# Sparse attention and an ELU layer on one core: x^T in the order of the tokens, local scores written with a step, output tiles of 128 neighbouring rows

## The chip, the cores and the metric

The kernel runs on one core of one Trainium2 chip. The metric is the device time of one execution in microseconds. Three runs of the kernel before gave 311.32 (median), 312.10 and 311.09 us. The profile of before is of one further execution, of 311.37 us.

## The reference

Eight batches of eight heads, 576 positions of 64 numbers each. The first four heads are local (a query sees itself and the 31 keys before it), the last four strided (a query sees the keys at or before it whose position has the same remainder by 32). The heads of a position are then put side by side to a row x of 512 numbers, and 4608 such rows go through two dense layers with an ELU between them.

```python
scores = scale * np.matmul(q, k.transpose(0, 1, 3, 2))
mask_local = (rel >= 0) & (rel < 32)
mask_strided = (rel >= 0) & (pos[None, :] % 32 == pos[:, None] % 32)
attn = np.exp(scores - max) / sum          # masked, per row
x = (attn @ v).transpose(0, 2, 1, 3).reshape(B * S, H * D)
h = x @ w_in                                # 512 -> 2048
g = np.where(h > 0, h, np.exp(np.minimum(h, 0.0)) - 1.0)
return g @ w_out                            # 2048 -> 512
```

Inputs and output are float32; the kernel computes its matmuls in bf16.

## The kernel before, in words

**Residues.** A batch's 576 positions are looked at as 72 groups p of NS = 8 neighbours s, position = 8p + s. Strided heads only mix positions of equal remainder by 8 (by 32 within it, by a mask), so their scores are eight blocks of 72 x 72 (RS = 72), one for each s. Local heads are cut into LB = 6 blocks of LQ = 96 queries, each against 128 keys (its own 96 and the 32 before).

**x^T.** The attention result is kept as `xT[128, 4, 4608]` in bf16, feature by token, all 4608 tokens in SBUF. Feature slices 0 and 1 are the local heads, 2 and 3 the strided. Within a batch its columns are in the order (s, p): column 72s + p holds position 8p + s. The dense layers don't mind the order of the tokens, so only the store has to undo it.

**Attention steps**, for a batch, a kind (s or l), a pair of heads y and a half u. T and c/C transpose q and k and copy them to `qT`, `kT` (batches from 3 on get them by a transposing DMA, X). q lies in `qT` in the order (s, p) for both kinds, keys of local heads in natural order. `scores` (S, L464) makes 8 matmuls of 72 columns (strided) or 6 of 96 columns (local), two at a time: one on rows 0 to 63 into one PSUM bank and one on rows 64 to 127 into another. Of a local block the 96 columns go to eight pieces of 12 neighbouring words (`local_cols`: order (s, block, p)). `exp_s` (e, L471, ScalarE) and `mask` (m, L478 strided, L484 local, VectorE) give the weights `pm`. `pv` (O) multiplies with V and with ones: for batches 0 and 1 in `pv_old` (L491 to L512), for the others in `pv_new` (L527 strided, L534 local; the local one reads and writes pieces of 12). `log_sums` and `recip` (n and r, L562 and L568, ScalarE) make 1 / sum as exp(-ln). `write_x` (x, L593, VectorE) multiplies the product in PSUM by it and writes x^T: 64 instructions, 32 strided that write contiguous columns and 32 local that write eight pieces of 36.

**Dense layers**, in nine chunks of 512 tokens. `l1` (a, b, L; L623): for each of 16 blocks of 128 hidden features, four matmuls of 512 columns over the feature slices in the order 2, 3, 0, 1. Then `exp_h` (h, L631, ScalarE), `clamp` (i on VectorE, L640, or j on ScalarE, L638), `elu` (g, L649 or L651, VectorE). `l2` (Z; L657): for each tile of 128 tokens, 16 matmuls of 512 columns over the hidden blocks. `copy_o` (o on ScalarE, q on VectorE; L663) brings the tile to SBUF, with four buffers, and `store` (t; L675) sends it to DRAM. The last tile is made in two halves of 256 columns (`l2_half` L683, `out_half` L696 to L700), whose last half goes out over SP and ACT.

**Stores.** A tile of 128 columns of x^T runs through two or three residues s, and the rows of one residue lie 8 rows apart in the output. So `store` sends each tile as 2 or 3 transfers, of up to 72 rows of 2 KB each.

**The order.** Nothing schedules itself: `ORDER` is a list of 1396 tokens written out ahead, each a step with its arguments (`S.3l1.0.34`: scores of batch 3, local, pair 1, half 0, into banks 3 and 4; `Z.2.1.0.2`: second layer of chunk 2, tile 1, quarter 0, bank 2). Every engine takes its instructions in that order, and waits by semaphores for operands, buffers and banks. All eight PSUM banks are given out by these tokens. Batch 0's attention comes first (the head), then stretches of first-layer blocks (h, i or j, g beside them) alternate with stretches in which second-layer quarters are mixed with the attention of later batches. q, k and v are loaded by POOL's queue (D), transposing DMAs (X) and stores share SP's queue.

Of the kernel before, what the change touches and what calls it, by code (L numbers as in the profile page):

```python
# [9 lines left out]
BF16 = mybir.dt.bfloat16  # L10
# [37 lines left out]
D.wo3.0 b.0.7 g.0.8 T.1s1.q.2 h.0.7 a.0.3.6 c.1s1.q T.1s0.k.1 C.1s0.q a.0.15.4 g.0.9 D.qs.2 C.1s0.k
T.1s1.k.2 i.0.7 b.0.15 c.1s1.k S.1s0.1.01 h.0.15 g.0.7 b.0.3 D.ks.2 e.1s0.1 b.0.14 i.0.15 h.0.3
g.0.15 T.1l1.q.7 S.1s0.0.01 h.0.14 m.1s0.1 S.1s1.0.45 D.ql.2 e.1s0.0 i.0.3 a.0.12.2 i.0.14 b.0.12  # L50
e.1s1.0 m.1s0.0 T.1l0.q.0 g.0.14 h.0.12 T.1l0.k.1 O.1s0.0.45 D.kl.2 C.1l0.q m.1s1.0 a.0.10.3 i.0.12
n.1s0.0 g.0.3 T.1l1.k.0 r.1s0.0 b.0.10 C.1l1.k x.1s0.0 a.0.13.6 g.0.12 h.0.10 O.1s0.1.45 C.1l0.k
c.1l1.q b.0.13 D.vs.2 V.1 n.1s0.1 S.1l1.0.12 h.0.13 Z.0.2.0.7 i.0.10 e.1l1.0 g.0.10 Z.0.1.0.0
r.1s0.1 m.1l1.0 j.0.13 x.1s0.1 S.1l0.1.12 g.0.13 O.1l1.0.34 D.vl.2 e.1l0.1 Z.0.2.1.7 n.1l1.0 m.1l0.1
r.1l1.0 Z.0.1.1.0 x.1l1.0 S.1l0.0.12 S.1s1.1.34 S.1l1.1.56 e.1l0.0 Z.0.2.2.7 e.1l1.1 m.1l0.0
Z.0.1.2.0 e.1s1.1 m.1l1.1 O.1l1.1.56 O.1l0.0.34 n.1l1.1 O.1s1.0.12 n.1l0.0 Z.0.2.3.7 m.1s1.1 n.1s1.0
r.1l0.0 r.1l1.1 Z.0.1.3.0 x.1l0.0 o.0.2 x.1l1.1 r.1s1.0 Z.0.0.0.3 t.0.2 o.0.1 x.1s1.0 Z.0.0.1.3
t.0.1 Z.0.0.2.3 Z.0.0.3.3 O.1s1.1.12 o.0.0 O.1l0.1.67 n.1s1.1 T.2s1.q.0 t.0.0 T.2s1.k.3 n.1l0.1
c.2s1.q r.1s1.1 T.2l0.k.5 c.2s1.k T.2l0.q.4 r.1l0.1 T.2l1.k.0 x.1s1.1 C.2l0.k T.2l1.q.3 x.1l0.1
S.2s1.0.12 C.2l1.k W.2 T.2s0.q.5 L.1.13.6 e.2s1.0 D.qs.3 c.2s0.q C.2l1.q c.2l0.q T.2s0.k.7 m.2s1.0  # L60
L.1.6.5 h.1.13 D.ks.3 V.2 j.1.13 c.2s0.k L.1.11.4 D.vs.3 h.1.6 g.1.13 D.ql.3 S.2s0.0.23 i.1.6 h.1.11
S.2l0.1.01 L.1.10.6 g.1.6 e.2s0.0 X.qs.3 i.1.11 e.2l0.1 L.1.8.7 m.2s0.0 h.1.10 g.1.11 O.2s0.0.01
h.1.8 L.1.5.2 m.2l0.1 i.1.10 n.2s0.0 i.1.8 O.2s1.0.34 X.ks.3 Z.0.3.0.5 g.1.10 r.2s0.0 g.1.8 h.1.5
Z.0.3.1.5 x.2s0.0 n.2s1.0 L.1.4.7 r.2s1.0 i.1.5 D.kl.3 g.1.5 L.1.7.6 h.1.4 x.2s1.0 Z.0.3.2.5 h.1.7
i.1.4 L.1.1.4 i.1.7 g.1.4 L.1.0.3 g.1.7 h.1.1 i.1.1 L.1.12.7 h.1.0 g.1.1 D.vl.3 X.ql.3 L.1.2.6 i.1.0
# [685 lines left out]
```

## Time and profile before

| | us |
|---|---|
| median of three runs | 311.32 |
| profiled execution | 311.37 |
| its span, first to last instruction | 309.4 |
| PE (matmuls) busy | 297.2 |
| ScalarE busy | 233.7 |
| VectorE busy | 223.4 |
| POOL busy | 74.8 |
| first-layer matmuls, L623 | 129.6 |
| second-layer matmuls, L657 | 128.9 |
| scores, L464, from 10 to 300 us | 15.2 |
| writes of x^T, L593 | 42.4 |

The span of a profile runs from the first to the last instruction of the core; what the execution takes beyond it lies around it. PE is TensorE's matmuls and PEld its weight loads, which overlap them; DVE is VectorE, ACT ScalarE, POOL GpSimd, SP SyncE, which here only issues DMAs. The durations of matmuls overlap too: one of 512 columns is shown with some 380 ns, while the next starts 216 ns later. So the cost of a matmul in a stream is read from the length of a row of several: its length less the duration of the last, by the number less one. A row of the timeline is start, length, engine, line, operation, tiles and shape, count, and in brackets how long the engine was idle before it and who released it. Some matmul records are missing in a trace.

### The profile page before, as it was taken

What the parts mean: (1) busy time and instruction counts of PE and PEld (TensorE: products, weight loads), DVE (VectorE), ACT (ScalarE), POOL (GpSimd) and SP (SyncE); (2) the same over time, 40 slices, a digit from 0 to 9 for tenths busy, and PEclk for the clock granted to TensorE, in tenths of its full rate; (3) what the DMA queues carried; (4) which work ended last, traced back from release to release, by engine and by line L of the source; (5) the groups of instructions that cost most, each with busy time, mean ns of one, the idle gap of its engine ahead of it and who ended that gap; (6) DMA issues with size and microseconds to landing.
All of it is one profiled execution on the core that took longest, in us unless ns stands there. A gap on an engine that the chain in (4) does not pass through costs nothing.

```text
span 309.4 us, 6379 instructions
## 1 busy us (share of the span) xinstructions
PE 297.2 (96%) x2374; PEld 151.6 (49%) x2412; DVE 223.4 (72%) x445; ACT 233.7 (76%) x410; POOL 74.8 (24%) x104
## 2 busy tenths in 40 slices
PE   5989999999999999999999999999999999999994
PEld 5754545544554455444544544455444544444443
DVE  6869972999669976898689679946798359990100
ACT  4769976979887899887998997879886767881211
POOL 8933310761084048003810082000000000000000
PEclk9559999999999999999999999999999999999999
DMA  8999999999999999994999589222200220002222
GB/s 161 189 206 206 195 206 213 165 133 152 151 200 161 123 201 183 106 125 87 190 155 122 119 113 159 47 67 71 68 3 0 70 68 1 0 2 57 67 79 70
DMA packets 96952, 36.29 MB, mean 117 GB/s; under 512 B 77754, under 2 KB 92442, under 8 KB 96922
## 3 DMA queue, kind: packets, MB, share of 16 engines
q0 software_dynamic: 64608, 19.40, 61.0%
q1 hardware_dynamic: 31878, 16.09, 28.9%
q10 hardware_dynamic: 436, 0.40, 0.5%
q8 instruction: 19, 0.31, 0.4%
q14 instruction: 11, 0.09, 0.1%
HBM read 39.41 MB, written 9.44 MB: 158 GB/s over the span
## 4 chain that ended last, share of the span: by engine, by line
PE 72%; DVE 15%; DMA 6%; issue 4%; ACT 2%; DVEq 0%; ACTq 0%
PE ps L657 34%; PE ps L623 27%; DVE g L651 6%; DMA vl<-in_v_dram 5%; DVE he L640 5%; PE ps L464 3%; PE ps L527 2%; PE ps L534 2%; DVE xT L593 1%; DMA g<-in_k_dram 1%; DVE g L649 1%; PE ps L683 1%; PE ps L421 1%; PE ps L418 1%; ACT he L631 1%
## 5 line engine op out<-in xcount | busy, mean ns | idle before, releaser
L623 PE MATMUL ps<-xT,w_in_sb 128*128 128x512 bf16 x560 | 129.6, 381 | 1.5 <-DVE g L651 0.4
L657 PE MATMUL ps<-w_out_sb,g 128*128 128x512 bf16 x538 | 128.9, 379 | 1.8 <-issue 1.0
L631 ACT ACTIVATE he<-ps 128x512 f32<-128x512 f32 x144 | 84.5, 594 | 23.3 <-PE ps L623 21.0
L623 PEld LDWEIGHTS <-w_in_sb 128*128 128x128 bf16 x576 | 55.1, 98 | 65.3 <-issue 2.3
L657 PEld LDWEIGHTS <-g 128*128 128x128 bf16 x560 | 50.6, 98 | 53.4
L651 DVE TENSOR_TENSOR g<-he,ps 128x512 bf16<-128x512 bf16 x112 | 74.0, 681 | 1.5
L640 DVE TENSOR_SCALAR he<-he 128x512 bf16<-128x512 f32 x112 | 46.3, 431 | 16.2 <-ACT he L631 15.7
L593 DVE TENSOR_TENSOR xT<-ps,ln 64x576 bf16<-64x576 f32 (+1 forms) x64 | 42.4, 678 | 21.6 <-ACT ln L568 21.1
L471 ACT ACTIVATE e<-ps 128x576 bf16<-128x576 f32 (+1 forms) x64 | 39.4, 646 | 5.8 <-PE ps L464 5.0
L562 ACT ACTIVATE ln<-ps 64x576 f32<-64x576 f32 (+1 forms) x64 | 36.3, 584 | 5.8 <-PE ps L527 2.6
L568 ACT ACTIVATE ln<-ln 64x576 f32<-64x576 f32 (+1 forms) x64 | 38.7, 620 | 1.4
L663 ACT COPY osb<-ps 128x512 f32<-128x512 f32 x27 | 15.8, 585 | 29.1 <-PE ps L657 26.1
L232 POOL DMA_DIRECT2D vs<-in_v_dram x8 | 5.3, 662 | 71.7 <-DVE vsp L603 69.4
L478 DVE TENSOR_TENSOR pm<-e,mask_s 72x576 bf16<-72x576 bf16 x32 | 14.4, 451 | 11.3 <-ACT e L471 10.8
L649 DVE SCALAR_TENSOR_TENSOR g<-he,ps 128x512 bf16<-128x512 bf16 x32 | 21.7, 680 | 0.6
L638 ACT ACTIVATE he<-he 128x512 bf16<-128x512 f32 x32 | 20.1, 627 | 0.7
L484 DVE TENSOR_TENSOR pm<-e,mask_l 128x576 bf16<-128x576 bf16 x32 | 14.5, 456 | 5.4 <-ACT e L471 4.4
L238 POOL DMA_DIRECT2D ql<-in_q_dram x20 | 16.3, 821 | 0.5 <-issue 0.4
L245 POOL DMA_DIRECT2D kl<-in_k_dram x20 | 15.5, 801 | 1.2 <-DMA vs<-in_v_dram 0.9
L527 PEld LDWEIGHTS <-vsp 72*128 72x128 bf16 x192 | 9.1, 98 | 5.8 <-DVE vsp L603 0.7
L700 DVE COPY osb<-ps 128x128 f32<-128x128 f32 x1 | 0.3, 291 | 15.0 <-ACT osb L699 15.0
L534 PEld LDWEIGHTS <-vl 128*128 128x128 bf16 x144 | 8.2, 97 | 4.4
(87 smaller groups left out, 176.4 us busy)
## 6 DMA issues: line engine op xcount, KB each, us to landing
out_dram<-osb SPq DMA_DIRECT2D x31, 144.0 KB
w_out_sb<-in_moe_w_out_dram POOLq DMA_DIRECT2D x4, 512.0 KB, 15.4
vl<-in_v_dram POOLq DMA_DIRECT2D x7, 288.0 KB, 6.6
qs<-in_q_dram POOLq DMA_DIRECT2D x5, 320.0 KB, 9.5
ks<-in_k_dram POOLq DMA_DIRECT2D x5, 320.0 KB, 11.2
vs<-in_v_dram POOLq DMA_DIRECT2D x5, 320.0 KB, 6.0
w_in_sb<-in_moe_w_in_dram POOLq DMA_DIRECT2D x3, 512.0 KB, 11.2
ql<-in_q_dram POOLq DMA_DIRECT2D x20, 72.0 KB, 6.9
```

What stands on the lines that cost most here:

```text
L238: nc.gpsimd.dma_start(out=t[0:RS, h % 2, :, h // 2, :], in_=q[b, h].rearrange("(p s) d -> p s d", s=NS))
L471: nc.scalar.activation(e[0:R], tiles.pop(("S", key, u))[0:R], ACT.Exp, scale=scale)
L562: nc.scalar.activation(t, s_ps, ACT.Ln)
L568: nc.scalar.activation(t, t, ACT.Exp, scale=-1.0)
L593: nc.vector.tensor_mul(dst, o_ps, rc)
L623: nc.tensor.matmul(tiles["h", ch, m], lhsT=w_in_sb[:, c, m * 128:(m + 1) * 128], rhs=xT[:, c, ch * CHUNK:(ch + 1) * CHUNK], start=(c == 2) ...
L631: nc.scalar.activation(e, tiles["h", i[0], i[1]], ACT.Exp)
L638: nc.scalar.activation(e1, e, ACT.Relu, bias=1.0, scale=-1.0)
L640: eng.tensor_scalar(e1, e, scalar1=1.0, scalar2=1.0, op0=ALU.min, op1=ALU.subtract)
L649: nc.vector.scalar_tensor_tensor(dst, e1, -1.0, h, op0=ALU.mult, op1=ALU.max)
L651: nc.vector.tensor_tensor(dst, e1, h, op=ALU.max)
L657: nc.tensor.matmul(ops, lhsT=g[ch % 2][:, m, kk * 128:(kk + 1) * 128], rhs=w_out_sb[:, m, :], start=(m == 0), stop=(m == MC - 1), skip_gro ...
```

## The change

1. `xT` holds a batch's tokens in natural order: column 8p + s. `write_x` of the strided heads writes `dst` with a step of 8 elements of bf16 (16 bytes), that of the local heads contiguous halves of 288.
2. Local scores, weights and products are in natural order. `local_cols` is a contiguous slice of 96, and only the scores' matmul writes with a step: eight runs over s, in each 12 words that lie 8 words (32 bytes) apart. The local mask is built in that order.
3. `store` sends a tile as one transfer of 128 neighbouring rows (the last half tile as two of 64 rows, from SP and ACT).
4. `ORDER` is made anew: the same steps, other places and other PSUM banks for many of them. It has the same 1396 tokens by kind, but for: one clamp from VectorE to ScalarE (111 i and 33 j, from 112 and 32), one output copy from VectorE to ScalarE (7 q and 28 o, from 8 and 27), two copies of transposes from ScalarE to VectorE (`c.1l0.q`, `c.1l1.k`). Which blocks' clamps run on ScalarE is chosen anew as well. The groups of scores with no other TensorE work between them are 36, from 37.

```diff
 ORDER: made anew; the stretch around the last local scores of batch 0, before and after
-D.vs.1 T.0l1.q.1 r.0s1.1 c.0l1.k O.0l0.1.67 n.0l0.0 r.0l0.0 c.0l1.q n.0l0.1 V.0.1 D.ql.1 S.0l1.1.01
-x.0l0.0 r.0l0.1 x.0s1.1 e.0l1.1 S.0l1.0.23 x.0l0.1 a.0.0.4 e.0l1.0 m.0l1.1 D.kl.1 O.0l1.1.67 m.0l1.0
+D.vs.1 T.0l1.q.1 n.0l0.1 r.0s1.1 c.0l1.q r.0l0.1 x.0s1.0 O.0l0.0.01 x.0l0.1 D.ql.1 S.0l1.0.67 V.0.1
+n.0l0.0 S.0l1.1.23 x.0s1.1 e.0l1.0 a.0.0.4 e.0l1.1 m.0l1.0 D.kl.1 r.0l0.0 O.0l1.0.67 m.0l1.1 x.0l0.0
...
-    mask_1 = consts.tile([128, NS, LN], BF16, tag="mask_1", name="mask_1")
-    mask_l = consts.tile([128, 2, NS, 3, LN], BF16, tag="mask_l", name="mask_l")
+    mask_1 = consts.tile([128, LQ], BF16, tag="mask_1", name="mask_1")
+    mask_l = consts.tile([128, 2, 3, LQ], BF16, tag="mask_l", name="mask_l")
...
     def local_cols(t, i):
-        return t.rearrange("k (s b p) -> k b s p", s=NS, b=3)[:, i]
+        return t[:, i * LQ:(i + 1) * LQ]
...
-                    dst = local_cols(sc[:, z], i)
+                    dst = local_cols(sc[:, z], i).rearrange("k (p s) -> k s p", s=NS)
...
-        n = RS // 2
-        if P.old:
-            xs = xT[:, P.y + c0, toks]
...
-        if not P.str:
-            o_ps = o_ps.rearrange("c x (s n) -> c x s n", s=NS)
-            rc = rc.rearrange("c x (s n) -> c x s n", s=NS)
+        xs = xT[:, P.y + c0:P.y + c0 + 1, toks] if P.old else xT[rows, c0:c0 + 2, toks]
+        h = NS // 2
+        if P.str:
+            dst = xs.rearrange("c x (n s) -> c x s n", s=NS)[:, :, int(u) * h:(int(u) + 1) * h]
+            o_ps = o_ps.rearrange("c x (s n) -> c x s n", s=h)
+            rc = rc.rearrange("c x (s n) -> c x s n", s=h)
+        else:
+            dst = xs[:, :, int(u) * W:(int(u) + 1) * W]
         nc.vector.tensor_mul(dst, o_ps, rc)
...
-    out_v = out.rearrange("(b p s) f -> b s p f", b=B, s=NS)
...
-        while c < c0 + 128:
-            b, r = divmod(c, S)
-            s, p = divmod(r, RS)
-            n = min(RS - p, c0 + 128 - c)
-            engs[i % len(engs)].dma_start(out=out_v[b, s, p:p + n, fs], in_=o_sb[c - c0:c - c0 + n, fs])
-            c, i = c + n, i + 1
+        c0, n = int(ch) * CHUNK + int(kk) * 128, 128 // len(engs)
+        for i, eng in enumerate(engs):
+            eng.dma_start(out=out[c0 + i * n:c0 + (i + 1) * n, fs], in_=o_sb[i * n:(i + 1) * n, fs])
```

More of the change, by code (lines that the diff above doesn't have):

```diff
@@ L48 @@
[L48 to L53, printed above, removed]
@@ new lines @@
+b.0.0 h.0.4 b.0.2 h.0.0 i.0.4 a.0.5.7 D.wo0.0 h.0.2 a.0.6.3 i.0.0 g.0.4 b.0.5 j.0.2 b.0.6 g.0.0
+h.0.5 a.0.8.6 h.0.6 g.0.2 a.0.11.4 b.0.11 i.0.5 j.0.6 D.wo1.0 b.0.1 g.0.5 h.0.11 a.0.9.5 g.0.6 h.0.1
+b.0.8 D.wo2.0 i.0.11 b.0.9 h.0.8 i.0.1 a.0.7.7 g.0.11 h.0.9 a.0.14.1 j.0.8 g.0.1 T.1s0.q.2 D.wo3.0
+b.0.7 C.1s0.q i.0.9 T.1s1.q.0 g.0.8 a.0.3.4 h.0.7 T.1s0.k.2 c.1s1.q j.0.7 a.0.15.6 D.qs.2 g.0.9
+T.1s1.k.0 C.1s0.k b.0.15 g.0.7 S.1s0.1.23 h.0.15 c.1s1.k b.0.14 D.ks.2 e.1s0.1 b.0.3 i.0.15 a.0.12.0
+h.0.14 g.0.15 S.1s0.0.23 h.0.3 m.1s0.1 S.1s1.0.67 D.ql.2 e.1s0.0 T.1l0.q.5 i.0.14 i.0.3 b.0.12
@@ new lines @@
+r.1l1.1 Z.0.2.3.0 x.1l0.0 o.0.1 x.1l1.1 r.1s1.0 Z.0.0.0.3 t.0.1 o.0.2 x.1s1.0 Z.0.0.1.3 t.0.2
+Z.0.0.2.3 Z.0.0.3.3 O.1s1.1.12 o.0.0 O.1l0.1.67 n.1s1.1 T.2s1.q.0 t.0.0 T.2s1.k.3 n.1l0.1 c.2s1.q
+r.1s1.1 T.2l0.k.5 c.2s1.k T.2l0.q.4 r.1l0.1 T.2l1.k.0 x.1s1.1 C.2l0.k T.2l1.q.3 x.1l0.1 T.2s0.q.1
+C.2l1.k W.2 L.1.6.2 D.qs.3 C.2l1.q c.2s0.q c.2l0.q L.1.8.0 h.1.6 V.2 T.2s0.k.1 h.1.8 i.1.6
+S.2s1.0.34 D.ks.3 c.2s0.k L.1.13.7 e.2s1.0 g.1.6 D.vs.3 i.1.8 S.2s0.0.56 h.1.13 S.2l0.1.34 m.2s1.0
+L.1.0.2 D.ql.3 e.2s0.0 g.1.8 X.qs.3 e.2l0.1 Z.0.3.0.1 m.2s0.0 i.1.13 h.1.0 m.2l0.1 O.2s0.0.34
@@ new lines @@
+Z.0.3.1.1 g.1.13 n.2s0.0 i.1.0 O.2s1.0.67 r.2s0.0 X.ks.3 g.1.0 L.1.7.0 n.2s1.0 x.2s0.0 L.1.1.2
+r.2s1.0 L.1.5.3 h.1.7 x.2s1.0 D.kl.3 h.1.1 L.1.10.4 i.1.7 h.1.5 i.1.1 g.1.7 L.1.15.7 h.1.10 g.1.1
+j.1.5 L.1.11.0 i.1.10 h.1.15 g.1.5 L.1.4.2 h.1.11 g.1.10 j.1.15 L.1.12.3 i.1.11 D.vl.3 h.1.4 g.1.11
+X.ql.3 Z.0.3.2.1 g.1.15 h.1.12 i.1.4 j.1.12 L.1.2.0 g.1.4 D.qs.4 L.1.14.7 g.1.12 h.1.2 i.1.2 L.1.3.2
+h.1.14 g.1.2 S.2l1.0.34 i.1.14 h.1.3 Z.0.3.3.1 X.kl.3 g.1.14 e.2l1.0 i.1.3 S.2s0.1.56 o.0.3
+S.2l1.1.34 m.2l1.0 L.1.9.7 e.2s0.1 g.1.3 D.ks.4 t.0.3 e.2l1.1 O.2l1.0.01 m.2s0.1 Z.1.0.0.2 h.1.9
@@ new lines @@
+m.2l1.1 n.2l1.0 i.1.9 O.2l1.1.34 O.2s0.1.56 g.1.9 n.2l1.1 Z.1.0.1.2 r.2l1.0 Z.1.0.2.2 r.2l1.1
+x.2l1.0 Z.1.0.3.2 n.2s0.1 x.2l1.1 r.2s0.1 S.3s0.1.01 q.1.0 S.2l0.0.34 Z.1.1.0.7 e.3s0.1 x.2s0.1
+t.1.0 e.2l0.0 Z.1.1.1.7 m.3s0.1 S.2s1.1.56 S.3s0.0.34 e.2s1.1 O.2l0.1.01 X.qs.4 Z.1.1.2.7 m.2l0.0
+n.2l0.1 m.2s1.1 Z.1.1.3.7 r.2l0.1 O.2s1.1.56 X.ks.4 e.3s0.0 x.2l0.1 Z.1.3.0.2 o.1.1 W.3 O.2l0.0.01
+n.2s1.1 Z.1.3.1.2 m.3s0.0 D.vs.4 r.2s1.1 t.1.1 O.3s0.1.34 D.ql.4 Z.1.2.0.7 n.2l0.0 x.2s1.1 n.3s0.1
+Z.1.2.1.7 r.2l0.0 O.3s0.0.56 r.3s0.1 x.2l0.0 Z.1.3.2.2 n.3s0.0 x.3s0.1 L.2.9.0 r.3s0.0 D.kl.4
@@ new lines @@
+D.kl.5 Z.2.1.0.7 e.4s1.1 m.3l1.1 o.2.0 m.4s1.1 S.4s0.0.01 S.4l1.0.56 S.3l0.0.34 e.4s0.0 t.2.0
+Z.2.1.1.7 e.3l0.0 m.4s0.0 O.3l1.1.01 e.4l1.0 m.3l0.0 O.4s0.0.23 Z.2.1.2.7 n.4s0.0 m.4l1.0 X.ql.5
+O.3l0.0.56 n.3l1.1 Z.2.1.3.7 D.vl.5 n.3l0.0 Z.2.2.0.4 r.4s0.0 q.2.1 r.3l0.0 Z.2.2.1.4 x.4s0.0 t.2.1
+D.qs.6 r.3l1.1 x.3l0.0 S.4l1.1.23 Z.2.2.2.4 e.4l1.1 x.3l1.1 O.4l1.0.23 X.kl.5 m.4l1.1 L.3.11.0
+D.ks.6 n.4l1.0 L.3.1.1 r.4l1.0 h.3.11 x.4l1.0 L.3.7.5 h.3.1 i.3.11 L.3.9.2 i.3.1 h.3.7 g.3.11 j.3.7
+L.3.0.3 g.3.1 h.3.9 g.3.7 L.3.14.0 h.3.0 i.3.9 L.3.15.1 i.3.0 h.3.14 g.3.9 j.3.14 L.3.8.5 g.3.0
@@ new lines @@
+e.4l0.0 m.4l0.1 O.4l1.1.67 Z.3.3.3.3 m.4l0.0 n.4l1.1 D.kl.6 O.4l0.1.45 r.4l1.1 q.3.3 S.5l1.0.12
+Z.3.1.0.0 e.5l1.0 x.4l1.1 t.3.3 n.4l0.1 S.5s0.1.12 m.5l1.0 S.5s1.1.67 Z.3.1.1.0 e.5s1.1 e.5s0.1
+m.5s1.1 O.4l0.0.67 Z.3.1.2.0 r.4l0.1 m.5s0.1 D.vl.6 X.ql.6 n.4l0.0 O.5s1.1.12 x.4l0.1 Z.3.1.3.0
+r.4l0.0 O.5s0.1.45 o.3.1 x.4l0.0 Z.3.2.0.3 n.5s0.1 t.3.1 L.4.2.0 r.5s0.1 L.4.1.6 D.qs.7 h.4.2
+x.5s0.1 X.kl.6 D.ks.7 n.5s1.1 L.4.9.7 i.4.2 g.4.2 h.4.1 L.4.0.4 h.4.9 i.4.1 g.4.1 L.4.4.0 r.5s1.1
+i.4.9 h.4.0 L.4.10.6 g.4.9 h.4.4 i.4.0 L.4.13.5 h.4.10 i.4.4 g.4.0 L.4.3.7 h.4.13 g.4.4 j.4.10
@@ new lines @@
+Z.4.1.0.3 n.5l0.0 m.5s1.0 X.ks.7 O.5s1.0.67 r.5l0.0 Z.4.1.1.3 W.6 n.5s1.0 Z.4.3.2.0 x.5l0.0 D.vs.7
+n.6l1.1 r.5s1.0 O.5l1.1.12 D.ql.7 Z.4.3.3.0 r.6l1.1 x.5s1.0 n.5l1.1 Z.4.1.2.3 x.6l1.1 r.5l1.1
+S.5l0.1.67 q.4.3 S.6l1.0.45 Z.4.1.3.3 e.5l0.1 x.5l1.1 t.4.3 e.6l1.0 D.kl.7 S.6s1.0.67 o.4.1 m.5l0.1
+S.6l0.0.01 S.6s0.0.45 m.6l1.0 Z.4.0.0.2 e.6l0.0 t.4.1 e.6s1.0 m.6l0.0 O.5l0.1.01 Z.4.2.0.3 n.5l0.1
+m.6s1.0 O.6l0.0.67 e.6s0.0 Z.4.0.1.2 n.6l0.0 m.6s0.0 D.vl.7 X.ql.7 O.6l1.0.45 r.5l0.1 Z.4.2.1.3
+r.6l0.0 x.5l0.1 Z.4.0.2.2 n.6l1.0 x.6l0.0 L.5.5.0 r.6l1.0 x.6l1.0 L.5.12.1 h.5.5 i.5.5 L.5.4.4
@@ new lines @@
+m.6s0.1 O.6s0.0.45 Z.5.3.0.0 o.4.2 m.7l0.1 e.7s0.0 t.4.2 O.6s0.1.23 n.6s0.0 m.7s0.0 O.7l0.1.67
+Z.5.3.1.0 n.6s0.1 n.7l0.1 Z.5.3.2.0 r.6s0.1 Z.5.3.3.0 r.7l0.1 x.6s0.1 r.6s0.0 Z.5.0.0.1 x.7l0.1
+o.5.3 x.6s0.0 S.7s1.0.67 S.6l0.1.23 e.7s1.0 Z.5.0.1.1 t.5.3 e.6l0.1 m.7s1.0 S.7l1.0.67 S.6s1.1.45
+m.6l0.1 S.7s1.1.23 e.7l1.0 Z.5.0.2.1 e.6s1.1 m.7l1.0 O.6l0.1.67 e.7s1.1 m.6s1.1 Z.5.0.3.1 n.6l0.1
+O.6s1.1.23 O.7l1.0.45 r.6l0.1 W.7 Z.5.1.0.0 n.6s1.1 x.6l0.1 Z.5.1.1.0 n.7l1.0 q.5.0 r.6s1.1
+O.7s0.0.67 Z.5.1.2.0 m.7s1.1 r.7l1.0 t.5.0 x.6s1.1 Z.5.1.3.0 n.7s0.0 x.7l1.0 r.7s0.0 L.6.2.1 o.5.1
@@ new lines @@
+h.8.10 i.8.12 g.8.12 L.7.10.7 h.8.3 i.8.10 L.8.6.1 i.8.3 h.7.10 g.8.10 L.8.0.6 i.7.10 h.8.6 g.8.3
+L.8.11.2 i.8.6 h.8.0 g.7.10 j.8.0 L.8.5.0 g.8.6 h.8.11 g.8.0 L.7.1.7 h.8.5 i.8.11 L.7.7.1 i.8.5
+h.7.1 g.8.11 L.8.2.6 g.8.5 h.7.7 i.7.1 L.7.8.2 h.8.2 i.7.7 g.7.1 L.7.2.0 h.7.8 i.8.2 g.7.7 L.8.7.7
+h.7.2 g.8.2 L.7.5.1 i.7.8 h.8.7 i.7.2 g.7.8 j.8.7 L.7.9.6 h.7.5 g.7.2 L.7.0.2 h.7.9 g.8.7 j.7.5
+i.7.9 L.7.4.0 h.7.0 g.7.5 L.7.6.7 h.7.4 g.7.9 i.7.4 L.7.11.1 h.7.6 i.7.0 g.7.4 L.7.13.6 h.7.11 i.7.6
+g.7.0 L.8.14.0 h.7.13 i.7.11 g.7.6 L.8.13.2 h.8.14 g.7.11 j.7.13 L.8.8.7 i.8.14 h.8.13 g.7.13
@@ new lines @@
+L.8.1.1 h.8.8 g.8.14 j.8.13 L.7.15.6 i.8.8 h.8.1 g.8.8 L.8.4.0 h.7.15 g.8.13 L.7.12.7 i.8.1 h.8.4
+i.7.15 g.8.1 L.7.3.5 h.7.12 g.7.15 j.8.4 Z.8.2.0.1 i.7.12 h.7.3 g.8.4 Z.8.0.0.6 i.7.3 g.7.12
+Z.8.2.1.1 g.7.3 Z.8.2.2.1 Z.8.2.3.1 Z.8.0.1.6 o.8.2 Z.7.0.0.7 t.8.2 Z.7.0.1.7 Z.7.0.2.7 Z.8.0.2.6
+Z.8.0.3.6 L.7.14.5 o.8.0 Z.7.2.0.6 t.8.0 h.7.14 i.7.14 Z.7.2.1.6 g.7.14 Z.7.2.2.6 Z.7.0.3.7
+Z.7.2.3.6 o.7.0 Z.7.3.0.7 t.7.0 o.7.2 Z.7.3.1.7 t.7.2 Z.7.3.2.7 Z.7.3.3.7 Z.7.1.0.6 o.7.3 Z.7.1.1.6
+t.7.3 Z.7.1.2.6 Z.7.1.3.6 Z.8.1.0.7 o.7.1 Z.8.1.1.7 t.7.1 Z.8.1.2.7 Z.8.1.3.7 o.8.1 t.8.1 Y.8.3.0.6
@@ L149 @@
+y.8.3.0 Y.8.3.1.0 y.8.3.1
 """
@@ L345 @@
         mask_1, mask_1, compare_op=ALU.is_ge, fill=0.0,
-        base=-1, pattern=[[-1, NS], [-NS, LN]], channel_multiplier=1)
+        base=-1, pattern=[[-1, LQ]], channel_multiplier=1)
     nc.gpsimd.affine_select(
         mask_1, mask_1, compare_op=ALU.is_ge, fill=0.0,
-        base=PRE, pattern=[[1, NS], [NS, LN]], channel_multiplier=-1)
+        base=PRE, pattern=[[1, LQ]], channel_multiplier=-1)
     def fill(what, eng=None):
@@ L364, in fill @@
                 nc.vector.tensor_copy(mask_l[:, u],
[L365 to L366 removed]
+                                      mask_1.unsqueeze(1).to_broadcast([128, 3, LQ]))
+            nc.vector.memset(mask_l[0:PRE, 0, 0, :], 0.0)
     class Pair:
```

165 lines of the change are left out of this document (48 added, 117 removed).

## The prediction

> **What bounds the kernel now.** I read the page's shares of busy time first, then the chain that ended last, then the busy time by stretch, then the timeline of TensorE around single runs of scores.
>
> ```profile
> span 309.4 us, 6379 instructions
> PE 297.2 (96%) x2374; PEld 151.6 (49%) x2412; DVE 223.4 (72%) x445; ACT 233.7 (76%) x410; POOL 74.8 (24%) x104
> ...
> PEclk9559999999999999999999999999999999999999
> ...
> PE 72%; DVE 15%; DMA 6%; issue 4%; ACT 2%; DVEq 0%; ACTq 0%
> ```
>
> TensorE is busy for 297.2 of 309.4 us, at the full granted clock but for about 8 to 22 us, and 72% of the chain lies on it. The idle rest is 12.2 us. The stretches say where:
>
> ```profile
> 15.20:18.60 3.40, 2.72 (x52) 2.20 (x48) 3.30 (x8) 3.22 (x10) 1.27 (x2) 0.50 1.30 205
> 18.60:22.02 3.42, 3.06 (x21) 1.44 (x21) 1.82 (x5) 2.12 (x5) 1.18 (x1) 0.50 1.24 207
> ...
> 126.00:139.00 13.00, 12.95 (x72) 6.03 (x72) 12.87 (x26) 11.71 (x21) 0.00 (x0) 1.00 1.23 111
> ...
> 199.00:220.50 21.50, 21.07 (x203) 11.11 (x206) 12.89 (x24) 18.60 (x33) 0.00 (x0) 1.00 0.22 62
> ```
>
> The columns are stretch, length, busy PE, PEld, DVE, ACT, POOL with counts, then the clock, DMA share and GB/s. In a stretch of first-layer matmuls (126 to 139) PE and DVE are both full; in one of second-layer matmuls and attention (199 to 220.5) PE is full and DVE has 8.6 us to spare. Over the ten stretches that I asked for between 20 and 302 us PE sums to 278.4 of 282 us. So no order of the same work can win more than 3.6 us there, and whatever a matmul grows by is paid in full.
>
> **The change part by part.** The profiled execution took 311.37 us, of which the span is 309.4 and 1.97 lie around it; the median of the three runs is 311.32, so both bases agree.
>
> Local scores (L464). The matmul count, the operands and the 96 columns stay, but neighbouring columns of the result now land 8 words (32 bytes) apart in PSUM, where before they fell in pieces of 12 neighbouring words. No row of this trace shows TensorE writing single words. The rows near it:
>
> ```profile
> 13.55 0.66 PE L464 MATMUL ps<-qTl,kTl 64*128 64x96 bf16 x12 [0.15 <-DVE kTl L439]
> ```
>
> ```profile
> 172.37 0.43 PE L464 MATMUL ps<-qTl,kTl 64*128 64x96 bf16 x12
> ```
>
> ```profile
> 118.58 0.67 PE L534 MATMUL ps<-pm,vl 128*128 128x96 bf16 x12
> ```
>
> Two matmuls of a pair (the upper and the lower 64 rows) run together into two banks. Twelve of them are six pairs. At full clock they take 0.43 us, the last alone 0.20 (the median duration of the line is 203 ns), so a pair costs (430 - 203) / 5 = 45 ns, 0.47 ns a column. At half clock a pair costs (660 - 270) / 5 = 78 ns, 0.81 ns a column. The third row writes the same 8 pieces of 12 words at (670 - 204) / 11 = 42 ns for 96 columns: pieces of 12 cost nothing. Scattered PSUM words show in the reads of another line, where the elements lie 144 bytes apart:
>
> ```profile
> L439 ACT COPY kTl<-ps 128x576 bf16<-128x576 bf16 x4 | 2.5, 648 | 0.0
> ...
> L435 DVE COPY qTs<-ps 128x576 bf16<-128x576 bf16 x4 | 1.8, 453 | 4.3 <-PE ps L418 4.3
> ...
> L439 DVE COPY kTl<-ps 128x576 bf16<-128x576 bf16 x2 | 1.5, 752 | 0.1
> ```
>
> VectorE reads 576 neighbouring elements in 453 ns and 576 scattered ones in 752: 299 ns more, 0.52 ns for each. The scattered reads thus give up what the neighbours shared. If TensorE's writes do too, a column goes from 0.42 to about twice that, which is the half-clock pace of 0.81 that the same matmul shows. I take 80 ns for a pair, 35 more than now. Keys of batches 1 to 7 have 7 x 2 pairs of heads x 2 halves = 28 batches of scores at full clock, 84 pairs: 84 x 35 = +2.9 us. Batch 0 runs at the half clock and pays nothing by this. The ends: nothing, if single words go as fast as pieces of 12; and 752 / 576 = 1.31 ns a word, with VectorE's fixed part in it, which makes 125 ns a pair, 84 x 80 = +6.7 us. Below nothing it can't go, since 96 columns at 0.42 ns are 40 of the 45 ns. I choose between the ends by the row with the same instruction.
>
> The Trainium skill bears on this (PSUM — Partial Sum Buffer, Specifications): it gives PSUM lines of 8 bytes and says that any non-contiguous pattern slows matmuls significantly. The row of 118.58 us speaks against "any", for its 48-byte pieces go at full pace; an 8-byte line holds two words, and single words would use half of each. By "any" taken literally the kernel already pays and the change would add nothing; by the lines it would cost what I take, and no run here shows which.
>
> One run of scores less. In the order, the groups of scores with no other TensorE work between them go from 37 to 36. Each run costs a gap on both sides, because it uses half the rows:
>
> ```profile
> 171.63 0.81 PE L657 MATMUL ps<-w_out_sb,g 128*128 128x512 bf16 x3 [0.16 <-issue]
> ```
>
> That is 0.16 us idle behind a run; with the weight load in front, which sits idle 12.3 us in 30 times for L464 by the waits (0.41 each, against 0.12 between two loads of a stream of 216 ns), I estimate 0.2 us a run: -0.2 us.
>
> Local products with V (L512, L534): contiguous instead of pieces of 12, at 42 ns already bound by their 96 columns: 0.
>
> Writes of x^T (L593). The 32 local writes become contiguous, the 32 strided ones now write single bf16 16 bytes apart.
>
> ```profile
> L593 DVE TENSOR_TENSOR xT<-ps,ln 64x576 bf16<-64x576 f32 x48 | 35.5, 753 | 17.5 <-ACT ln L568 17.1
> ...
> L593 DVE TENSOR_TENSOR xT<-ps,ln 128x288 bf16<-128x288 f32 x16 | 6.9, 452 | 4.1 <-ACT ln L568 4.0
> ```
>
> Each group holds both kinds, half of it contiguous and half in pieces of 36, between 739 and 762 ns, so pieces cost nothing, and (753 - 452) / 288 is 1.05 ns an element, one at a time already; the scattered reads of L439 go at that pace too (752 for 576). No row shows scattered writes to SBUF. The ends: 0, and twice the pace, +600 ns on 24 writes and +300 on 8, 16.8 us of VectorE. I take 0, by the L439 row. The other end is rival C.
>
> Stores (L675). 98 transfers (97 from SP, 1 from ACT) become 38 of whole 128-row tiles; an issue takes 0.36 us in the middle, so SP saves some 20 us. By the waits only one instruction ever waits for a store, a copy of L663, once, for 2.9 us (281.0 to 283.9), where PE is full. DMA is down to 0.22 busy in stretches such as 199 to 220. The last tile still ends on one transfer from SP and one from ACT. I count 0; if a copy waits longer for a buffer, it has four of them as cover, and costs TensorE only when an output bank is late.
>
> Order and banks. One clamp (431 ns on VectorE, 627 on ScalarE) and one output copy (689, 585) go from VectorE to ScalarE, two copies of transposes (446 and 752 on VectorE, 645 and 646 on ScalarE) come back: VectorE +0.08 us, ScalarE -0.08. In the head the vl copy stands one place earlier on VectorE, in front of a mask product; its transfer was issued at 5.4 us and lands in about 6.6, so it is there before 13 us: no new wait. TensorE's counts stay. The rest is bank choice, of which I can only bound the worth: up to 3.6 us to gain (all idle from 20 to 302 us), and, as VectorE is full in the first-layer stretches, about as much to lose. I take 0 and +-0.9.
>
> Sum: 311.37 + 2.9 - 0.2 = **314.1 us**.
>
> **The rivals.**
>
> B, single words are as free as pieces of 12 (the row of 118.58 us speaks for it: 42 ns for 96). Then 311.4 - 0.2 = 311.2, between 310.3 and 312.1 with the order's 0.9. This is also the case in which the change does nothing to the time.
>
> C, the scattered writes to SBUF go at half pace. VectorE has room for 2.1 us a batch in a stretch like 199 to 220 (8.6 us free), but the last write before a chunk stands in front of its first matmul, and then VectorE is full. That makes 0.6 us late at each of the seven borders to chunks 1 to 7: +4.2, so 315.4 without the scores' price and 318.3 with it. It decides from a write of about 1.3 us on. For it: nothing but that no row excludes it. The Trainium skill has a rule for it (SBUF — State Buffer, the note on cachelines under its port table): SBUF lines of 16 bytes, of which an engine should hit each at least twice, while it calls a step of 8 bf16 free. Each write of the change hits a new line, so its two halves disagree here, and no run here shows which holds.
>
> D, the worst end of the scores: +6.7 - 0.2, 317.9. For it only the 1.31 ns with a fixed part in it.
>
> E, faster than before: the head warms sooner. The granted clock is 0.5 until 22.02 us. In 15.20 to 18.60 PE is idle 0.68 us, 0.4 of it as a score run waits for L593 and 0.2 for the copy of q; the new order gives batch 0's last local scores other banks (67 and 23) and copies q before it writes x^T. If PE is full there and the clock comes back one step of 3.4 us sooner, at 18.6, the 3.06 us of work that PE does from 18.60 to 22.02 take half: -1.5 us, 311.2 - 1.5 = 309.7 if the scores pay nothing (312.6 if they do). It decides from a full stretch on; against it, PE still lacks VectorE's results there.
>
> **How the numbers follow.** About 0.3% (0.93 us) is what a measurement of this kernel tells from no change, so the borders are 310.4 and 312.3. Chances: the forecast 0.50 (313.0 to 315.2), B 0.28, C 0.10, D 0.04, E 0.08. Of B, 0.06 are faster, 0.16 within, 0.06 slower, as the order's share falls; of the forecast, 0.01 within. So faster 0.14 (0.06 + 0.08), same 0.17, slower 0.69 (0.49 + 0.06 + 0.10 + 0.04). The range leaves out E, the low end of B and the top of C and D: 310.4 to 318.0. The forecast is slower because the one matmul that changes lies on the full engine, and nothing that gets lighter does.
>
> **What would show it.** The twelve-matmul rows of local scores at full clock: 0.43 us would be (430 + 5 x 35), about 0.6, for the forecast, 0.43 for B, 0.8 for D; those of batch 0 stay at 0.66, since half a clock hides the price, which tells a limit of the memory from one of the array. Strided writes of x^T stay at 753 and 452 ns; 1350 is C. The granted clock at 18.6 us is E. SP's issues fall to 37 without a change in the end of the chain. I am wrong if local scores keep their time and the span still moves by over 1 us: then the order did it, and PE's idle time between 20 and 302 us, 3.6 us now, must show it.

## The result, and the profile after

The kernel after takes 357.38 us (median of four runs), the one before 311.71: 1.141 times as long, with a 95% interval of 1.129 to 1.153. By this ratio it is 44 us more (45.7 by the medians), where the forecast was +2.7 and its range ended at 318.0. The profiled execution of after took 356.87 us. The ratios are of means and leave out runs more than 1.5% above the fastest of their kernel: one of these four, and two of the four of the run with the stepped write alone below.

The page of after: the busy time, then TensorE and VectorE in 40 slices, then the chain by engine and by line.

```profile
span 355.2 us, 6329 instructions
...
PE 312.8 (88%) x2412; PEld 156.3 (44%) x2412; DVE 273.5 (77%) x445; ACT 235.0 (66%) x410; POOL 74.5 (21%) x104
...
PE   5879999969878978898898978998679899999995
...
DVE  5877974999799977699869977985899947996100
...
PE 55%; DVE 23%; ACT 10%; issue 7%; DMA 3%; DVEq 0%; ACTq 0%
PE ps L614 26%; PE ps L648 20%; DVE xT L584 15%; ACT ln L562 4%; PE ps L464 4%; ACT ln L568 3%; DVE g L642 3%; DVE he L631 2%; ACT e L471 1%; DMA g<-in_k_dram 1%; PE ps L534 1%; DMA qTs<-qs 1%; PE ps L418 1%; ACT he L622 1%; DVE osb L654 1%
```

The row of TensorE before:

```profile
PE   5989999999999999999999999999999999999994
```

TensorE has holes now: its row of nines shows eights, sevens and sixes in the stretches that hold attention, and its share of the chain falls from 72% to 55%. VectorE has 50.1 us more to do with the same 445 instructions, and one line of it, the write of x^T (L584 here, L593 before), is 15% of the chain. The groups, with count, busy time and mean duration:

```profile
L584 DVE TENSOR_TENSOR xT<-ps,ln 64x576 bf16<-64x576 f32 x48 | 81.7, 1764 | 15.4 <-ACT ln L568 14.8
...
L584 DVE TENSOR_TENSOR xT<-ps,ln 128x288 bf16<-128x288 f32 x16 | 14.5, 982 | 3.6 <-ACT ln L568 3.5
```

Before, these means were 753 and 452 ns, and both kinds of heads alike. Instruction by instruction, after has the local writes mostly where they were (from 739 and 446 ns on), and the strided ones at 2.70 to 2.91 us (24 of 576 elements, mean 2726 ns) and 1.42 to 1.66 us (8 of 288, mean 1462). That is 24 x 1.97 + 8 x 1.01 = 55 us more by their durations; the 50.1 us of the page count a stretch in which two instructions overlap once. Who waits for them, by the waits of after (engine, line, releaser: us in total, times, longest):

```profile
PE ps L464 <- DVE xT L584: 15.1, 12, 1.9
...
PE ps L614 <- DVE xT L584: 11.3, 9, 3.0
...
PE ps L527 <- DVE xT L584: 2.8, 2, 1.8
```

Before, the only such wait was one of 0.4 us. Scores and products wait for the PSUM banks that a write of x^T reads, and the first layer for x^T itself: 29.2 us in all. One case in the timeline:

```profile
239.97 2.72 DVE L584 TENSOR_TENSOR xT<-ps,ln 64x576 bf16<-64x576 f32 x1 [1.74 <-ACT ln L568]
...
241.07 0.42 PE L464 MATMUL ps<-qTl,kTl 64*128 64x96 bf16 x6
...
242.75 0.44 PE L464 MATMUL ps<-qTs,kTs 64*128 64x72 bf16 x16 [1.25 <-DVE xT L584]
...
243.09 1.19 ACT L471 ACTIVATE e<-ps 72x576 bf16<-72x576 f32 x2 [1.33 <-PE ps L464]
```

The write runs to 242.69. TensorE stands for 1.25 us in front of the next scores, and ScalarE for 1.33 us behind them. The middle row is the other cost: six local scores take 0.42 us. Before they took 0.30:

```profile
171.17 0.30 PE L464 MATMUL ps<-qTl,kTl 64*128 64x96 bf16 x6
```

By the starts of the single matmuls in the trace, pairs of local scores behind the first two of a row follow each other at 81 to 84 ns in after, against 41 to 44 before.

### The profile page after: what moved, and what is told of

It reads as the page before. It is cut to its first block, busy times and chain, and to the rows that moved or that the text cites. A ratio compares the mean times of both kernels' runs of the same rounds, so it can differ in the third digit from the quotient of the medians.

```text
span 355.2 us, 6329 instructions
## 1 busy us (share of the span) xinstructions
PE 312.8 (88%) x2412; PEld 156.3 (44%) x2412; DVE 273.5 (77%) x445; ACT 235.0 (66%) x410; POOL 74.5 (21%) x104
## 4 chain that ended last, share of the span: by engine, by line
PE 55%; DVE 23%; ACT 10%; issue 7%; DMA 3%; DVEq 0%; ACTq 0%
PE ps L614 26%; PE ps L648 20%; DVE xT L584 15%; ACT ln L562 4%; PE ps L464 4%; ACT ln L568 3%; DVE g L642 3%; DVE he L631 2%; ACT e L471 1%; DMA g<-in_k_dram 1%; PE ps L534 1%; DMA qTs<-qs 1%; PE ps L418 1%; ACT he L622 1%; DVE osb L654 1%
## 5 line engine op out<-in xcount | busy, mean ns | idle before, releaser
L614 PE MATMUL ps<-xT,w_in_sb 128*128 128x512 bf16 x576 | 133.7, 383 | 11.9 <-DVE xT L584 11.3
L648 PE MATMUL ps<-w_out_sb,g 128*128 128x512 bf16 x560 | 134.0, 383 | 0.2 <-DVE g L642 0.2
L584 DVE TENSOR_TENSOR xT<-ps,ln 64x576 bf16<-64x576 f32 (+1 forms) x64 | 96.2, 1569 | 19.0 <-ACT ln L568 18.4
L471 ACT ACTIVATE e<-ps 72x576 bf16<-72x576 f32 (+1 forms) x64 | 39.5, 646 | 25.9 <-PE ps L464 24.2
L631 DVE TENSOR_SCALAR he<-he 128x512 bf16<-128x512 f32 x111 | 45.7, 429 | 13.6 <-ACT he L622 13.1
L640 DVE SCALAR_TENSOR_TENSOR g<-he,ps 128x512 bf16<-128x512 bf16 x33 | 22.5, 682 | 0.7 <-ACT he L629 0.4
L464 PE MATMUL ps<-qTl,kTl 64*128 64x96 bf16 x192 | 14.4, 304 | 8.6 <-DVE xT L584 8.2
L464 PE MATMUL ps<-qTs,kTs 64*128 64x72 bf16 (+1 forms) x256 | 9.6, 204 | 7.4 <-DVE xT L584 6.9
L464 PEld LDWEIGHTS <-kTl 64*128 64x128 bf16 x192 | 8.5, 125 | 15.0 <-issue 14.1
## 6 DMA issues: line engine op xcount, KB each, us to landing
w_in_sb<-in_moe_w_in_dram POOLq DMA_DIRECT2D x3, 512.0 KB, 11.3
```

Of the source, the lines that this page charges most:

```text
L464: nc.tensor.matmul(dst, lhsT=P.kT[pr, k0:k0 + M], rhs=rhs, start=True, stop=True, skip_group_check=True)
L471: nc.scalar.activation(e[0:R], tiles.pop(("S", key, u))[0:R], ACT.Exp, scale=scale)
L584: nc.vector.tensor_mul(dst, o_ps, rc)
L614: nc.tensor.matmul(tiles["h", ch, m], lhsT=w_in_sb[:, c, m * 128:(m + 1) * 128], rhs=xT[:, c, ch * CHUNK:(ch + 1) * CHUNK], start=(c == 2) ...
L631: eng.tensor_scalar(e1, e, scalar1=1.0, scalar2=1.0, op0=ALU.min, op1=ALU.subtract)
L640: nc.vector.scalar_tensor_tensor(dst, e1, -1.0, h, op0=ALU.mult, op1=ALU.max)
```

## The experiments

My theory after the result: the single bf16 values written 16 bytes apart make VectorE slow, and that is nearly all of it. The rivals: the new order and banks, the scores' step, the stores, or a stepped write that disturbs other engines. Each median is given beside that of the kernel before on the same chip.

**One thing at a time, on the kernel before.** First the stepped write alone; tokens of the two kinds then don't match.

```diff
...
-                dst = xs[:, :, int(u) * W:(int(u) + 1) * W]
+                dst = xs.rearrange("c x (n s) -> c x s n", s=NS)[:, :, 4 * int(u):4 * int(u) + 4]
...
```

> The kernel before, with one thing of the change: the strided heads' writes of x^T go to natural columns (step of 8 bf16). Order, banks, scores and stores are those of before, so the tokens of the two kinds of heads no longer match and the output is not the reference's. If the stepped write is the cause (my theory now): 24 writes of 753 ns become 2726 and 8 of 452 become 1462 as in the profile of after, 55 us more of VectorE, and the time goes up by 35 to 45 us, to 345 to 357. If the order and banks are the cause (rival): those writes are as long, but the order of before hides them, under +10 us. If the scores' step or the stores are the cause: within 1 us of before.

Measured: a median of 356.09 us beside 311.9, and a ratio of 1.131 (1.124 to 1.139), which is +41 us. The rivals fall as main cause: in the order of before, with its scores and stores, +41 us is there.

The scores' step alone:

```diff
-                    dst = local_cols(sc[:, z], i)
+                    dst = sc[:, z, i * LQ:(i + 1) * LQ].rearrange("k (p s) -> k s p", s=NS)
```

> The kernel before, with the local scores' matmuls alone writing PSUM with a step of 8 words; masks, products and the rest as before, so weights and queries no longer match and the output is not the reference's. By the profile of after a pair of matmuls takes 83 ns against 43: 84 pairs at full clock x 40 ns = 3.4 us and 12 pairs of batch 0 x 80 ns = 1 us, so +3 to +4.5 us, to 314.5 to 316. If the step disturbs the neighbouring matmuls as well (the change of tiling behind a run takes longer): +6 us. If the rows of after only look longer because TensorE waits there for VectorE: within 1 us of before.

Measured: 314.86 beside 311.9, ratio 1.0093 (1.0061 to 1.0125), +2.9 us, a little under the expected range. In the head the twelve scores of batch 0 show this (the timeline of TensorE in this run, then in after):

```profile
14.13 1.14 PE L464 MATMUL ps<-qTl,kTl 64*128 64x96 bf16 x12 [0.16 <-DVE kTl L439]
```

```profile
15.59 1.14 PE L464 MATMUL ps<-qTl,kTl 64*128 64x96 bf16 x12
```

It was 0.66 us before. The granted clock in the head is 0.50 in before and after; this run's profile has no record of it there. By the starts in the trace of after, five of the six pairs follow each other at 160 ns there, against some 80 before. The step costs at half the clock as well, and twice as much, so it isn't a memory of fixed pace that limits it.

The order alone (before's forms, after's `ORDER`):

> The kernel before in every instruction's form, with the order and PSUM banks of after. If the stepped write is the cause: within 1 us of before (one run of scores less is worth 0.2 us). If the new order and banks are the cause: +20 us or more.

Measured: 312.37 beside 311.9, ratio 1.0022 (0.9995 to 1.0049): no difference that these runs can tell.

The stores alone:

```diff
...
-            engs[i % len(engs)].dma_start(out=out_v[b, s, p:p + n, fs], in_=o_sb[c - c0:c - c0 + n, fs])
...
+            eng.dma_start(out=out[c0 + i * n:c0 + (i + 1) * n, fs], in_=o_sb[i * n:(i + 1) * n, fs])
```

> The kernel before with the stores of after: one transfer of 128 neighbouring rows for each tile, 38 transfers instead of 98; x^T stays in the order of before, so the rows of the output are permuted. Nobody waits for SP, so within 0.5 us of before. If fewer transfers help the loads or the last landing: -0.5 to -1.5 us.

Measured: 311.47 beside 311.9, ratio 0.9992 (0.9974 to 1.0009): again no difference that can be told. By their ratios the four parts add up to 41.0 + 2.9 + 0.7 - 0.3 = 44.3 us, against 44 for the whole change.

**Is it the length alone?** Contiguous writes made long by repeating them, on the kernel before:

```diff
         nc.vector.tensor_mul(dst, o_ps, rc)
+        if P.str:
+            for i in range(2):
+                nc.vector.tensor_mul(dst, o_ps, rc)
+            if not P.old:
+                nc.vector.tensor_mul(dst[:, 0:1], o_ps[:, 0:1], rc[:, 0:1])
```

> The kernel before with each strided write of x^T made long without a step: it is written three times over, and one more time by half for batches 2 to 7, all contiguous and idempotent. That adds 24 x about 1.85 us and 8 x about 0.8 us, 51 us of VectorE, against 55 in the run with the step. If the length of the writes on VectorE is all that counts: +35 to +45 us. If the stepped write does more than occupy VectorE (it slows the reads of PSUM or SBUF of the other engines): clearly less, under +25.

Measured: 358.3 beside 312.26, ratio 1.152 (1.146 to 1.158). Slightly over the range of the theory, and no sign of a disturbance by the step: 46 us without any. The length of the writes is enough. Half of it, each strided write done twice:

> The kernel before with each strided write of x^T done twice, contiguous: 24 x 0.72 + 8 x 0.41 = 20.6 us more of VectorE. How much of added VectorE time ends in the time: 10.6 us gave about 3 (the run with runs of 4), 51 gave 46. If VectorE has a fixed room of some 8 us and the rest counts in full: +12. If it counts in proportion (0.85): +17.5. If it has more room at this order: under +6.

Measured: 324.96 beside 311.65, ratio 1.0435 (1.0408 to 1.0463), +13.3 us; the fixed room gave +12, the proportion +17.5. VectorE is busy 245.0 us there, 21.6 more than before, and 275.6 us in the longer one, 52.2 more. So 21.6 us end as 13.3 and 52.2 as 46: some 6 to 8 us find room, and the rest counts nearly in full, though VectorE was idle for 86 us of the span. From the shorter to the longer run 30.6 us of VectorE even bring 32.7 us. In the longer one the granted clock falls (0.66 in the mean from 101 to 106 us, 0.57 from 135 to 143, 0.72 from 250 to 256), in the shorter one it is 1.00 from 20 to 320 us. That is worth up to 5 x 0.34 + 8 x 0.43 + 6 x 0.28 = 6.8 us of TensorE's work; without them the room is up to 13 us.

**What the step costs by itself.** Single operations behind the kernel's end, four of each on VectorE and ScalarE, 24 of each matmul.

> The kernel before with single operations measured by themselves behind its end (the time of the whole says nothing): VectorE products of 576 elements from PSUM written as bf16 with steps of 1, 2, 4, 8, 16 and 32 elements, in runs of 2 and 4 every 16 bytes, as fp32 with steps of 1, 2, 4, with scattered reads; copies and ScalarE copies with such steps; matmuls of 96 columns written to PSUM with steps of 1, 2, 4 and 8 words, in aligned and unaligned pairs of words. If what costs is a new 16-byte line for each element: 753 ns up to a step of 4, 2.7 us from a step of 8 on, fp32 slow at a step of 4, runs of 4 in between. If what costs is a part of a word written alone: 2.7 us from a step of 2 on, fp32 free at any step. For matmuls by an 8-byte line: 42 ns for step 1 and for aligned pairs, 83 for all steps from 2 on; unaligned pairs between.

The groups of that run. L737 to L747 write 576 bf16 with steps of 1, 2, 4, 8, 16 and 32 elements; L751 writes runs of two and L754 runs of four, every 16 bytes; L757 to L761 write fp32 with steps of 1, 2 and 4. In L768 the PSUM operand is read 144 bytes apart, in L770 the one in SBUF.

```profile
L743 DVE TENSOR_TENSOR xT<-ps,one 64x576 bf16<-64x576 f32 x4 | 10.8, 2700 | 0.1
L747 DVE TENSOR_TENSOR xT<-ps,one 64x576 bf16<-64x576 f32 x4 | 10.6, 2649 | 0.1
L745 DVE TENSOR_TENSOR xT<-ps,one 64x576 bf16<-64x576 f32 x4 | 10.3, 2579 | 0.1
...
L741 DVE TENSOR_TENSOR xT<-ps,one 64x576 bf16<-64x576 f32 x4 | 5.8, 1458 | 0.1
...
L761 DVE TENSOR_TENSOR w_in_sb<-ps,one 64x576 f32<-64x576 f32 x4 | 4.6, 1162 | 0.1
...
L770 DVE TENSOR_TENSOR xT<-ps,one 64x576 bf16<-64x576 f32 x4 | 4.5, 1123 | 0.1
...
L739 DVE TENSOR_TENSOR xT<-ps,one 64x576 bf16<-64x576 f32 x4 | 3.2, 797 | 0.1
L751 DVE TENSOR_TENSOR xT<-ps,one 64x576 bf16<-64x576 f32 x4 | 3.0, 749 | 0.1
L754 DVE TENSOR_TENSOR xT<-ps,one 64x576 bf16<-64x576 f32 x4 | 3.0, 749 | 0.1
L759 DVE TENSOR_TENSOR w_in_sb<-ps,one 64x576 f32<-64x576 f32 x4 | 3.0, 749 | 0.1
...
L768 DVE TENSOR_TENSOR xT<-ps,one 64x576 bf16<-64x576 f32 x4 | 3.0, 744 | 0.1
L737 DVE TENSOR_TENSOR xT<-ps,one 64x576 bf16<-64x576 f32 x4 | 2.9, 733 | 0.1
```

Neither law that I had written fits alone. Halving the step from 8 to 4 saves 1242 ns, from 4 to 2 another 661: beside a fixed 0.2 us (2700 - 2 x 1242) an element costs 4.3, 2.2 and 1.0 ns, and larger steps than 8 cost no more. So the price is for each 16 bytes that are entered. But it is high only where part of a 4-byte word is written alone: runs of two bf16, each pair filling one word of its 16 bytes, are free (pairs that start in the middle of a word were not tried), and fp32 with one word in 16 bytes costs (1162 - 749) / 576 = 0.7 ns an element more, not 3.4. Scattered reads of PSUM cost this product nothing, scattered reads of fp32 in SBUF about as much as scattered fp32 writes. ScalarE follows the same rows with steps of 2, 4 and 8:

```profile
L792 ACT CAST g<-ps 64x576 bf16<-64x576 f32 x4 | 10.8, 2710 | 0.1
...
L790 ACT CAST g<-ps 64x576 bf16<-64x576 f32 x4 | 5.8, 1460 | 0.1
...
L788 ACT CAST g<-ps 64x576 bf16<-64x576 f32 x4 | 3.2, 800 | 0.1
```

The matmuls of 96 columns followed each other at 42 to 43 ns with contiguous words, with aligned pairs of words every 32 bytes and with a right operand in pieces, and at 82 to 83 ns with steps of 2, 4 and 8 words and with pairs that start on an odd word (starts in the trace, 24 of each, at a granted clock of 1.00). A right operand read with a step of 4 bf16 costs too: 86 to 87 ns.

**Taking the step away.** The loop of the strided write turned round, so that it writes runs of 4 bf16 and scatters its reads:

```diff
-            dst = xs.rearrange("c x (n s) -> c x s n", s=NS)[:, :, int(u) * h:(int(u) + 1) * h]
-            o_ps = o_ps.rearrange("c x (s n) -> c x s n", s=h)
-            rc = rc.rearrange("c x (s n) -> c x s n", s=h)
+            dst = xs.rearrange("c x (n s) -> c x n s", s=NS)[:, :, :, int(u) * h:(int(u) + 1) * h]
+            o_ps = o_ps.rearrange("c x (s n) -> c x n s", s=h)
+            rc = rc.rearrange("c x (s n) -> c x n s", s=h)
```

> The kernel after with one loop turned round: the strided heads' write of x^T goes through the residue s innermost, so it writes runs of 4 bf16 (8 bytes) and scatters its reads of PSUM and of the reciprocals instead. Output and everything else as in after. If the single bf16 writes 16 bytes apart are what VectorE is slow at: the write falls from 2726 ns to between 753 (scattered reads are free, as for the copies of k) and 1300, and the time from 357 to 315 or 325 (the scores' step of 3 us stays). If reaching a new 16-byte line in each step is what costs, whichever side it is on: the writes stay above 2 us and the time above 345. If the order is to blame: no change.

Measured: 318.42 beside 312.26, ratio 1.021 (1.018 to 1.025). By the ratios, 37 of the 44 us are gone by three lines, with the order of after untouched. The write of 576 elements is at 1.15 us at most, near the 1123 ns of the single operation whose SBUF operand is read scattered, as the reciprocals are here:

```profile
L584 DVE TENSOR_TENSOR xT<-ps,ln 64x576 bf16<-64x576 f32 x48 | 44.3, 942 | 17.3 <-ACT ln L568 16.8
```

With the scores in pieces of 12 again and all 64 writes scattering their reads:

> The kernel after with no stepped write at all: the strided writes of x^T as in the run with runs of 4, local scores, masks and products in the pieces of 12 of before, and the local writes of x^T contiguous with their reads scattered. Output as in after, in natural order, stores of whole tiles. If the two stepped writes are all that the change costs and scattered reads are free: 311 to 313. If scattered reads of the reciprocals in SBUF (fp32, 144 bytes apart) cost VectorE a half more: 48 writes of about 1.1 us, 317 to 325.

Measured: 323.28 beside 312.26, ratio 1.037 (1.034 to 1.040), in the case of the slow reads: 48 writes with a mean of 1146 ns and VectorE at 243.7 us, 20.3 more than before, for 11 us. Last, the scattering moved to where it was free, ln's read of PSUM:

```diff
-        nc.scalar.activation(t, s_ps, ACT.Ln)
+        nc.scalar.activation(t.rearrange("c x (n s) -> c x n s", s=k),
+                             s_ps.rearrange("c x (s n) -> c x n s", s=k), ACT.Ln)
...
-            rc = rc.rearrange("c x (s n) -> c x n s", s=h)
+            rc = rc.rearrange("c x (n s) -> c x n s", s=h)
```

> Natural order and whole-tile stores without any stepped write, in the order and banks of before: scores and products in pieces of 12, ln reads the sums in PSUM scattered and writes them in natural order, so that the reciprocals are read without a step, and the write of x^T scatters only its read of PSUM (744 ns measured for that, against 1124 with the reciprocals scattered). Output as in the reference's order by construction. If the law of the single operations holds in the kernel: 64 writes at 753 and 452 ns, ln at 643 and 411, and a time within 0.3% of before, 311 to 313, perhaps 0.4 us below it by the stores. If ScalarE pays for its scattered reads: ln above 800 ns and the time above 314.

Measured: 311.81 beside 311.65, ratio 1.0005 (0.9990 to 1.0021). The writes and ln in it:

```profile
L588 DVE TENSOR_TENSOR xT<-ps,ln 64x576 bf16<-64x576 f32 x48 | 35.5, 752 | 17.5 <-ACT ln L570 17.1
...
L563 ACT ACTIVATE ln<-ps 64x576 f32<-64x576 f32 x48 | 30.0, 642 | 3.5 <-PE ps L527 2.6 <-PE ps L534 0.2
```

Both are as before, where ln had this row:

```profile
L562 ACT ACTIVATE ln<-ps 64x576 f32<-64x576 f32 x48 | 30.0, 642 | 3.5 <-PE ps L527 2.6 <-PE ps L534 0.2
```

So x^T in natural order costs nothing that can be told if no engine writes parts of words and the scattered reads are those of PSUM. The same in the order and banks of after:

> The same in the order and banks of after. 311.5 to 313.5; within 0.3% of the other one.

Measured: 312.01 beside 311.65, ratio 1.0016 (1.0001 to 1.0032), at the edge of what can be told. No version is faster than the kernel before.

## Why the prediction was wrong

**What bounds the kernel** was read rightly only for TensorE. From VectorE's 8.6 idle us in a stretch of 21.5 I took room for 2.1 us a batch, some 15 us in all. The runs show 6 to 8, or up to 13 without the clock's share. The waits show why idle time elsewhere on VectorE does not help: scores and products wait 17.9 us for the bank that a write gives back, the first layer 11.3 us for x^T. But a room of 15 us would not have saved the forecast from 50 us of added work.

**The step that failed is the writes of x^T**: "No row shows scattered writes to SBUF. The ends: 0, and twice the pace", with 0 taken "by the L439 row". That row reads scattered PSUM. The runs show the product free of a price for such reads (744 against 733 ns), while scattered bf16 writes to SBUF take 3.6 times as long (2726 against 753): a read was no near row for a write, nor PSUM for SBUF, and the upper end of twice was not worked out from any row. Rival C had the slow write, with a chance of 0.10, but with 1.35 instead of 2.73 us for it and one write late at each chunk, 4.2 us; measured alone it is 41. Its place, in front of a chunk's first matmul, is right for the 11.3 us of the first layer's waits; the 17.9 us of waits for banks it did not have. My range ended just below C's 318.3, so it left out the cost that no row bounded instead of widening for it.

**Local scores**: a pair costs 80 to 83 ns as I took, and the whole step +2.9 us as forecast (1.9 to 3.9 by the interval). The close agreement is in part luck: by the rows 84 pairs pay 40 ns each and the 12 of batch 0 some 80, which is 4.3 us. "Batch 0 runs at the half clock and pays nothing" is wrong: 1.14 against 0.66 us for twelve. Matmuls that write words singly take twice as long as contiguous ones at either clock (83 against 42 ns, 160 against 80 a pair); the pace of 0.8 ns that the half-clock row lent me was the right number for another reason. D is out.

The Trainium skill (PSUM — Partial Sum Buffer, Specifications) gives PSUM lines of 8 bytes and says any non-contiguous pattern slows matmuls. The lines agree with the run: 83 ns for single words and for pairs across two lines, 42 for aligned pairs. "Any" does not: aligned pairs every 32 bytes go at full pace.

The Trainium skill (SBUF — State Buffer, the note on cachelines under its port table) asks for two hits on a 16-byte line and calls a step of 8 bf16 free. Here the measurement decides against it, for writes: a step of 8 takes 2700 ns against 733, a step of 4, with two hits on each line, 1458, and one run of two bf16 in each line is free (749).

**One run of scores less, order and banks**: worth nothing that can be told, as forecast (1.0022, 0.9995 to 1.0049). **Stores**: 0, as forecast; SP issues 37 instead of 97. **Local products**: no cost to be seen, as forecast (a mean of 206 ns in after against 204); no run tests them alone.

**E** did not come, though its condition did. In after TensorE is busy for all 3.40 us from 15.20 to 18.60, but only for 2.03 of the next 3.42, and the granted clock is 0.50 until 25.40 and 0.58 from there to 28.80; in before it was 1.00 from 22.02 on. It falls again later (0.91 in the mean from 110 to 150 us, 1.00 in before), around a stretch in which TensorE is busy only 6.99 of 10 us (125 to 135). By the spans and mean clocks TensorE loses 355.2 x 0.038 = 13.5 us of work against 309.4 x 0.023 = 7.1, so up to 6.4 of the 44 us come by way of the clock, which the prediction had only as a gain. The clock falls in the run with repeated writes too, so it takes no step; that holes in TensorE's work bring it down is argued, not shown by a run of its own.

What stays open is why part of a word costs 4.3 ns for each 16 bytes; no run here shows it.

## What to carry to other kernels

When an edit gives an access pattern that no row of the trace shows, measure that instruction by itself before pricing the edit: here reads told nothing of writes, nor PSUM of SBUF. Where an order has to be changed, scatter the read of PSUM and keep the writes in whole words; runs of two bf16 that fill a word are enough. Try that read first as well: it was free for this product and for ln, but VectorE's bf16 copy of L439 takes 752 ns where one in order takes 453. An engine that is 72% busy may have room for some 10 us of 300 only, if its instruction gives a bank or an operand back.

## What the runs showed of the hardware that I had not expected

- bf16 written by VectorE or ScalarE to SBUF singly, with gaps: about 4.3 ns for each 16 bytes entered (797, 1458, 2700 ns for 576 elements with steps of 2, 4, 8; 733 without, 632 on ScalarE). Runs of two or four, filling whole words: 749.
- fp32 with one word in 16 bytes: 1162 ns written by VectorE, 1182 by ScalarE, 1123 when a scattered fp32 operand is read from SBUF. Scattered fp32 reads of PSUM in such a product: 744.
- Matmuls that write words singly to PSUM take 83 ns for 96 columns against 42, and a pair of them 160 ns against 80 at half the granted clock. Aligned pairs of words every 32 bytes take 42.
